# A scheduled attention-plus-scan kernel: the third bank of a three-bank score tile may be lent to VectorE, and the plan's seeds are drawn anew

## The chip, the core and the metric

The kernel runs on one core of one Trainium2 chip. The metric is the device time of one execution in microseconds (us): 775.2 us is the median of the three runs before the change (774.59 to 775.41). Five engines run side by side, each with its own queue: TensorE (PE in the profile), VectorE (DVE), ScalarE (ACT), GpSimd (POOL) and SyncE (SP), which here only issues DMAs.

## What is computed

Two independent layers over 2048 positions and 640 channels, whose outputs stand side by side. A is a diagonal complex state-space layer, B an attention with 32 query heads of width 20 that share one key and one value head:

```
A:  h = Lam_bar * h + B_bar @ x[t];  y[t] = 2 * Re(C @ h) + Dskip * x[t]
B:  q = (x @ wq) in 32 heads of 20;  k = x @ wk;  v = x @ wv
    p = softmax(q k^T / sqrt(20));   out = (p v, heads joined) @ wo
out = concat(A, B)
```

## The kernel before

**The bulk of the work is the exponential.** Attention is cut into 32 groups (4 blocks of 512 queries, 8 groups of 4 heads each). A group has 64 units; a unit is one head's 512 queries against 128 keys: a 128x512 tile of scores that needs an exponential. That makes 2048 units. A unit goes one of two ways:

- **By ScalarE.** TensorE writes two or three units into one PSUM tile, `R0` (three banks) and `R1` (two banks) in turn (`TILES = (3, 2)`), and one ACTIVATE with Exp (line 1243) turns the whole tile into bf16 probabilities in `P`. One PV matmul a unit then adds to `PV`.
- **By VectorE, a "D unit".** TensorE writes one unit into a bank of its own, `B0` or `B1`. One tensor_scalar (`dx_op`, line 1248) adds an offset, clamps at zero and converts to int16, whose bits read as bf16 approximate the exponential. Three shifted copies (`sh_op`, line 1253), each over up to three units, and four PV matmuls, with value rows scaled for each shift, average the error out. So a D unit costs VectorE one pass out of PSUM and three in SBUF, and TensorE four PV matmuls where a ScalarE unit needs one.

PSUM has eight banks: three for `R0`, two for `R1`, one for `PV`, and two for `B0` and `B1`. Those two B banks are shared by the D units and by every other matmul that needs PSUM: the query projections, the state-space input products (`sa`, lines 870 to 890), the state-space outputs (`sy`, y_tile, whose 13 or 12 matmuls hold one bank from the first to the last), and the output projection (`proj`).

**The order of instructions is made by a planner in the kernel file** when it is built. `main` keeps a clock for each engine and a list of candidates: the next fill of `R0` or `R1` ("fill"), the next exponential ("ex"), the next D unit ("dx"), shifts ("sh"), PV matmuls ("pv") and the heads of some background threads ("bg"). Each is offered with the time at which it could begin, plus a bias and some noise; the smallest goes next. Each operation then waits, on the chip, for the semaphores of the buffers that it reads and writes (`Plan.deps`), so a plan that is wrong about a duration shows up as a wait.

A fill may take a D unit with it. `want_d` decides: it wants the next of nine `Pd` slots to be free, a free B bank (`bank(None)`), no background thread that has waited for a bank longer than its patience (`starved`), VectorE's backlog below a limit, and the bank ready in time. `owner` tells for each of the two B banks who holds it; `d_group` allows 16 D units a group. `pick` chooses the units, `fill_op` makes the matmuls: 32 key rows each and three or four side by side, or, where two units stand alone, two of 64 rows. `R0c` is the dependency key of the third bank of `R0`; a three-unit fill and a three-unit exponential write and read both `R0` and `R0c`, and a two-unit one only `R0`.

The limits, patience and noise are drawn anew 64 times over the work by `vary`, from `random.Random(seed)` with the list `SEEDS`. Changing one entry, or one draw in `vary`, changes the whole order behind it.

Of the kernel before, what the change touches and what calls it, by code (L numbers as in the profile page):

```python
# [9 lines left out]
ALU = mybir.AluOpType  # L10
# [203 lines left out]
def dve_t(n, rate=1.0):  # L214
    return n / (960.0 * rate) + 0.07
# [28 lines left out]
class _Kernel:  # L244
# [17 lines left out]


    TURNS = 64
    SEEDS = (1006, 2007, 3008, 4004, 5008, 6003, 0, 8008, 9006, 0, 11003, 0, 13002, 14008, 0, 16002, 17003,
# [3 lines left out]

    def __init__(self, nc, t):  # L270
        self.nc, self.t = nc, t
# [21 lines left out]
    def alloc(self):  # L293
# [3 lines left out]
                  for i, n in enumerate(self.TILES)]  # L297
        self.PV = self.scope.enter_context(nc.psum_tensor("PV", [128, 512], FP32))
        self.BB = self.scope.enter_context(nc.psum_tensor("B", [128, 512 * self.BANKS], FP32))
        self.B = [self.BB[:, 512 * i:512 * i + 512] for i in range(self.BANKS)]  # L300
        self.p.psum.update(["R0", "R0c", "R1", "R1b", "PV", *(f"B{i}" for i in range(self.BANKS))])
        self.sb("xbT", [128, NC, S], BF16)
        self.sb("KT", [128, 2, S], BF16)
# [798 lines left out]
    def vary(self, seed):  # L1102

        r = self.rng = random.Random(seed)
        self.backlog = r.choice((2.5, 3.0, 3.5, 4.0, 5.0))
        self.spared = r.choice(((0.02, 0.02, 0.02), (0.05, 0.15, 0.02), (0.1, 0.3, 0.02), (0.02, 0.3, 0.02)))
        self.after = r.choice((0.1, 0.15, 0.2)), r.choice((0.35, 0.4, 0.5))
        self.few, self.wait, self.noise = r.choice((1, 1, 2)), r.choice((0.15, 0.25, 0.35)), r.choice((0.0, 0.05, 0.1))

        self.starved = dict(sy=r.choice((0.0, 1.0, 4.0, 99.0)), sa=r.choice((2.0, 99.0)),  # L1110
                            proj=r.choice((0.0, 1.0, 4.0, 99.0)),
                            qt=r.choice((0.0, 1.0, 4.0, 99.0)))
        self.open, self.first = r.choice((0.6, 0.7)), r.choice(("sy", "proj", None))

    def main(self):
        K, p = self, self.p
        NG = self.NQB * self.NGG
# [30 lines left out]
        def scan_open():  # L1148
# [2 lines left out]
        self.normed, self.projected, self.dense = set(), set(), set()  # L1151
        rest = self.rest
        done = lambda k=None: all(x == 64 for x in taken) and not any(k in (None, n % 2) for n, _ in tiles)
        fins = self.last_ops([lambda: done(0), lambda: done(1), lambda: done() and cur["raw"] == NG and not (any(owner) or sy or norm or proj),
                              lambda: done() and cur["raw"] == NG],
                             lambda gg: NG - self.NGG + gg in self.normed and not (gg == self.NGG - 1 and sy))
        threads = [("rest", rest), ("norm", norm), ("dense", dense), ("proj", proj), ("qt", qt), ("qr", qr), ("sy", sy), ("sa", sa), ("su", su), ("sr", sr), ("sc", sc_), ("sx", sx), *fins]
        owner = [None, "rest"]
        rest[-1].done = lambda: owner.__setitem__(1, None)
        holds, since = {}, {}  # L1160

        def bank(o):

            f = [i for i in range(2) if owner[i] is None]
            if not f:
                return None
            return min(f, key=lambda i: p.begin("pe", (), (f"B{i}",)))
# [6 lines left out]
        def pick(size, with_d):  # L1174

            g = next(i for i in range(NG) if taken[i] < 64)
            out, d = [], None
            heads = set()
            if size == 2 and not with_d and sum(len(x) for x in left[g]) > 8:
                for i in (0, 2):  # L1180
                    out.append((g, max((i, i + 1), key=lambda j: (bool(left[g][j]), -made(g, j), (taken[g] // 5 + j) % 2))))
                if all(left[g][j] for _, j in out):
                    return out, d
                out = []
            if with_d:
                gd = d_group(g)
                j = min(range(4), key=lambda j: (dcount[gd][j], made(gd, j), -len(left[gd][j])))
                if left[gd][j]:
                    d = (gd, j)
                    heads.add(j)  # L1190
            for gx in (g, g + 1):
                if gx >= NG or gx not in qt_done:
                    break
                for j in sorted(range(4), key=lambda j: (made(gx, j), -len(left[gx][j]), (j - taken[gx]) % 4)):
                    if j not in heads and left[gx][j] and len(out) < size:
                        out.append((gx, j))
                        heads.add(j)
            return out, d
# [13 lines left out]
                g += 1  # L1212
            return g if g < NG and g in qt_done and sum(dcount[g]) < self.QUOTA else None

        def want_d(g, t, n_tile):
            if not (g > 0 or taken[g] >= 24) or d_group(g) is None:
                return False
            if dunit_left.get(cur["d"] - self.DUNITS, 0) or bank(None) is None:
                return False
            if any(owner) and any(t - x > self.starved[name] * (name != "qt" or len(self.qsent) > 0) for name, x in since.items()):  # L1220
                return False
            return (backlog(t) <= self.backlog - 0.5 * n_tile
                    and p.begin("pe", (), (f"B{bank(None)}",)) <= t + self.spared[n_tile])

        def fill_op(n, out, d):
            lst, reads, writes = [], set(), ([f"R{n % 2}"] if out else []) + ["R0c"] * (len(out) == 3)
            units = list(out) + ([d] if d else [])
            wide = len({j // 2 for _, j in units}) == len(units)
            for i, (g, j) in enumerate(units):
                kc = left[g][j][-1]  # L1230
                lo, n_rows = (64 * (j // 2), 64) if wide else (32 * j, 32)
                dst = K.B[bank(None)][:, :] if i == len(out) else K.R[n % 2][:, 512 * i:512 * i + 512]
                lst.append(self.m1(dst, K.KT[lo:lo + n_rows, j % 2, 128 * kc:128 * kc + 128],
                                   K.QT[lo:lo + n_rows, g % self.QRING, :], True, True, (lo, 0), len(units)))
                reads |= {f"KT{j % 2}_{kc // 4}", f"QT{g % self.QRING}"}
            if d:
                writes.append(f"B{bank(None)}")
            return self.mms(lst, sorted(reads), writes, kind="QK")

        def ex_op(n, size):  # L1240
# [4 lines left out]

        def dx_op(n):
            u, x = n % self.DUNITS, holds[n]
            return Op("dve", lambda e: e.tensor_scalar(K.Pd[:, 0, u, :], K.B[x][:, :], self.d_off, 0.0, op0=ALU.add,  # L1248
                                                       op1=ALU.max), [f"B{x}"], [f"Pd{u}_0"], occ=dve_t(512))

        def sh_op(us, i):
            a, b = us[0][0], us[-1][0] + 1
# [38 lines left out]
        while True:  # L1291
# [8 lines left out]
            def offer(kind, o, bias, thread=None, arg=None):  # L1300
                cand.append((p.begin(o.eng, *o.keys(), o.accum) + bias + self.noise * self.rng.random(), len(cand), kind, o, thread,
                             arg))
# [3 lines left out]
            if cur["fill"] < cur["act"] + 2 and any(x < 64 for x in taken) and not early:  # L1306
                n = cur["fill"]
                g = next(i for i in range(NG) if taken[i] < 64)
                if g in qt_done:
                    t = p.begin("pe", (), (f"R{n % 2}",))  # L1310
                    out, d = pick(self.TILES[n % 2], want_d(g, t, n % 2))
                    o = fill_op(n, out, d)
                    t_fill = p.begin("pe", o.reads, o.writes)
                    t_fill = (t_fill, t_fill + self.after[n % 2])
                    offer("fill", o, -self.noise, arg=(out, d))
                    t = p.clock["pe"]
                    if d is None and want_d(g, t, 2):
                        d = pick(0, True)[1]
                        if d:
                            offer("fill", fill_op(n, [], d), 0.2, arg=([], d))  # L1320
            full = bool(tiles) and tile_left.get(tiles[0][0] - self.PTILES, 0) > 0
            if tiles:
                n, out = tiles[0]
# [80 lines left out]
                if o.done is not None:  # L1404
                    o.done()
            elif kind == "fill":
                out, d = arg
                self.units += len(out) + (d is not None)
                if out:
                    n = cur["fill"]  # L1410
# [5 lines left out]
                if d:  # L1416
                    g, j = d
                    taken[g] += 1
                    dcount[g][j] += 1
                    due[g][j] += 3  # L1420
                    dunits.append((cur["d"], (g, j, left[g][j].pop())))
                    holds[cur["d"]] = int(o.writes[-1][1])
                    owner[holds[cur["d"]]] = "D"
                    cur["d"] += 1
            elif kind == "ex":
# [80 lines left out]
```

## Time and profile before

| what | value |
|---|---|
| median of 3 runs | 775.2 us (774.59 to 775.41) |
| the profiled execution, its own time | 775.14 us |
| its span, first to last instruction | 773.2 us (1.9 us lie around it) |
| ScalarE busy | 757.0 us, 98% of the span |
| VectorE busy | 702.4 us, 91% |
| TensorE matmuls busy | 697.5 us, 90% |
| GpSimd busy | 441.0 us, 57% |
| exponentials (line 1243) | 325 of three banks, 328 of two |
| D units (line 1248) | 417, at 683 ns |
| shifts (line 1253) | 522, at 530 ns on average |
| granted TensorE clock | 0.989 |

Busy times are unions: two overlapping instructions of one engine count once. The mean of a group is that of an instruction from its own start to its own end, so overlapping ones have means that add up to more than the busy time. "Idle before" is the engine's idle time ahead of an instruction, with what ended it. Windows are in us from the start of the span.

### The profile page before, as it was taken

Reading aid. Unit: us, or ns where it says so; the run is one execution under the profiler, and the core shown is the slowest. Engines: PE = TensorE matmul, PEld = TensorE weight load, DVE = VectorE, ACT = ScalarE, POOL = GpSimd, SP = SyncE. Lnnn points to the kernel's source line nnn. Section 1 sums busy time; section 2 is a strip of 40 time slices with the busy share of each in tenths; the row PEclk is TensorE's granted clock in tenths of the full one; section 3 lists DMA queues with packets and bytes.
Section 4 is the critical chain, followed back from the end, with each engine's and each line's share of the span. In section 5 each row is a group of like instructions: output and inputs, shape, how many; then the busy total and the mean of one; then the engine's idle time right before and its main releaser. Section 6 shows DMA issues by size and latency. Waiting matters only on the chain.

```text
span 773.2 us, 16569 instructions
## 1 busy us (share of the span) xinstructions
PE 697.5 (90%) x6495; PEld 213.1 (28%) x6495; DVE 702.4 (91%) x1232; ACT 757.0 (98%) x686; POOL 441.0 (57%) x865
## 2 busy tenths in 40 slices
PE   5899887888889999998899999988899999889988
PEld 1322222222223333222223333222233332233323
DVE  6689999999997989899999788999989899998986
ACT  7999999999999999999999999999999999999995
POOL 4705753699997212499865300599992489940040
PEclk9799999999999999998999999999999999999999
DMA  8466101000020000210002010310000211000010
GB/s 186 86 149 132 38 15 49 16 16 15 1 57 29 30 23 32 51 50 15 15 10 61 30 40 17 65 42 23 2 23 22 62 40 38 2 19 21 28 42 35
DMA packets 61146, 31.49 MB, mean 41 GB/s; under 512 B 41478, under 2 KB 61070, under 8 KB 61070
## 3 DMA queue, kind: packets, MB, share of 16 engines
q1 hardware_dynamic: 58928, 30.12, 15.4%
q8 instruction: 52, 0.85, 0.5%
q10 hardware_dynamic: 2142, 0.32, 0.3%
q14 instruction: 24, 0.20, 0.1%
HBM read 9.21 MB, written 12.69 MB: 28 GB/s over the span
## 4 chain that ended last, share of the span: by engine, by line
ACT 69%; POOL 10%; DVE 10%; PE 8%; SPq 1%; issue 1%; DMA 1%; DVEq 0%; POOLq 0%
ACT P L1243 69%; POOL tm L906 4%; DVE Pd L1253 4%; POOL W L906 3%; PE R L418 3%; DVE Pd L1248 3%; PE PV L418 3%; PE B L418 2%; POOL uh L906 2%; SPq L399 1%; DVE hh L917 1%; DVE tm L890 1%; DMA xbT<-in_B_x_dram 1%; POOL tm L847 0%; DVE mabs L529 0%
## 5 line engine op out<-in xcount | busy, mean ns | idle before, releaser
L1243 ACT ACTIVATE P<-R 128x1536 bf16<-128x1536 f32 (+1 forms) x653 | 739.2, 1421 | 3.3 <-PE B L418 1.1
L1248 DVE TENSOR_SCALAR Pd<-B 128x512 int16<-128x512 f32 x417 | 282.3, 683 | 32.3 <-PE B L418 29.2
L418 PE MATMUL R<-QT,KT 32*128 32x512 bf16 (+1 forms) x1631 | 257.5, 389 | 56.7 <-ACT P L1243 42.7
L1253 DVE TENSOR_SCALAR Pd<-Pd 128x1536 int16<-128x1536 int16 (+2 forms) x522 | 259.9, 530 | 1.2
L418 PE MATMUL PV<-P,VP 128*32 128x512 bf16 x1631 | 256.2, 389 | 0.8 <-DVE Pd L1248 0.4
L418 PE MATMUL PV<-Pd,VP 128*32 128x512 bf16 x1668 | 252.6, 386 | 3.0 <-DVE OTr L1286 2.1
L906 POOL TENSOR_TENSOR tm<-hh,cs 128x128 bf16<-128x128 f32 x320 | 164.8, 537 | 23.4 <-DVE hh L917 8.9
L418 PE MATMUL B<-QT,KT 32*128 32x512 bf16 x417 | 161.6, 388 | 0.0
L418 PEld LDWEIGHTS R<-QT,KT 32*128 32x128 bf16 (+1 forms) x1631 | 64.1, 91 | 298.1 <-ACT P L1243 268.4
L906 POOL TENSOR_TENSOR W<-tm 128x128 bf16<-128x128 bf16 x160 | 91.9, 597 | 89.8 <-PE B L418 85.9
L906 POOL TENSOR_TENSOR uh<-tm 128x128 bf16<-128x128 bf16 x160 | 81.1, 527 | 63.7 <-DVE tm L890 59.6
L418 PEld LDWEIGHTS PV<-Pd,VP 128*32 128x32 bf16 x1668 | 59.1, 94 | 64.4 <-issue 38.3
L418 PEld LDWEIGHTS PV<-P,VP 128*32 128x32 bf16 x1631 | 59.2, 94 | 61.0 <-issue 45.9
L1000 POOL TENSOR_TENSOR OTd<-OTd,rwide 128x128 bf16<-128x128 bf16 x80 | 33.7, 448 | 67.8 <-DMA OTd<-o_rows 65.9
L890 DVE TENSOR_TENSOR tm<-B,cs 128x1024 bf16<-128x1024 f32 x40 | 48.5, 1213 | 3.6 <-PE B L418 3.4
L418 PE MATMUL B<-CGre,W 128*128 128x384 bf16 (+1 forms) x160 | 46.5, 305 | 0.8 <-POOL W L906 0.8
L418 PE MATMUL B<-CGim,W 128*128 128x384 bf16 (+1 forms) x160 | 45.6, 299 | 0.0
L847 POOL TENSOR_SCALAR tm<-W,sc 128x128 f32<-128x128 bf16 x40 | 30.7, 779 | 20.0 <-DVE CGre L849 12.5
L917 DVE TENSOR_TENSOR_SCAN hh<-sc,hini,uh 128x512 f32<-128x512 f32 x30 | 39.5, 1318 | 0.0
L418 PEld LDWEIGHTS B<-QT,KT 32*128 32x128 bf16 x417 | 37.8, 91 | 0.0
L418 PE MATMUL B<-xaT,BTim 128*128 128x512 bf16 x100 | 30.4, 384 | 0.6 <-DVE tm L890 0.4
L418 PE MATMUL PV<-cs,VP 128*128 128x512 bf16 x88 | 30.5, 390 | 0.0
(149 smaller groups left out, 414.1 us busy)
## 6 DMA issues: line engine op xcount, KB each, us to landing
o_rows<-OTr SPq DMA_DIRECT2D x32, 128.0 KB, 1.7
QT<-q_rows SPq DMA_DIRECT2D x30, 128.0 KB, 2.2
q_rows<-Qd SPq DMA_DIRECT2D x16, 160.0 KB, 2.8
OTd<-o_rows SPq DMA_DIRECT2D x16, 160.0 KB, 3.2
out_dram<-ystage SPq DMA_DIRECT2D x16, 160.0 KB, 1.8
out_dram<-ostage SPq DMA_DIRECT2D x12, 160.0 KB, 1.8
P<-in_B_wq_dram SPq DMA_DIRECT2D x1, 800.0 KB, 5.9
WO<-in_B_wo_dram SPq DMA_DIRECT2D x4, 200.0 KB, 3.5
```

Source lines behind the costliest of these rows:

```text
L399: return e.dma_start_transpose(out_ap, in_ap)
L418: ins = e.matmul(o() if callable(o) else o, lhsT=l, rhs=r, start=st, stop=sp, skip_group_check=True, **kw)
L847: pool(lambda e, y=y, c=c, gy=gy, i=i: e.tensor_scalar(K.ctmp[:, i:i + 128], y[:, i:i + 128], sc[:, gy, c:c + 1], None, op0=ALU.mult), key ...
L890: dve(lambda e, k=k, h=h: e.tensor_tensor(K.tm[:, 2 * k:2 * k + 2, :], bass.AP(tensor=K.BB, offset=512 * int(h.key[1]), ap=[[512 * self.BA ...
L906: put(lambda e, c0=c0, end=end: e.tensor_tensor(out[:, c0:end], a[:, c0:end], b[:, c0:end], op), reads, [writes + h], n, gate=None if i el ...
L917: dve(lambda e, ri=ri, ini=ini: e.tensor_tensor_scan(K.hh[:, ri, :], dec, K.uh[:, ri, :], ini, ALU.mult, ALU.add), ["sc", *(f"uh{ri}{h}" f ...
L1000: ops.append(Op("pool", lambda e, c=c, m=m: e.tensor_tensor(K.OTd[:, m, c], K.OTd[:, m, c], K.rwide[:, c], ALU.mult), rw + [f"OTe{dd}" for ...
L1243: return Op("act", lambda e: e.activation(dst, K.R[n % 2][:, 0:512 * size], ACT.Exp, scale=self.exp_scale), [f"R{n % 2}"] + ["R0c"] * (siz ...
L1248: return Op("dve", lambda e: e.tensor_scalar(K.Pd[:, 0, u, :], K.B[x][:, :], self.d_off, 0.0, op0=ALU.add, op1=ALU.max), [f"B{x}"], [f"Pd{ ...
L1253: return Op("dve", lambda e: e.tensor_scalar(K.Pd[:, i, a:b, :], K.Pd[:, 0, a:b, :], float(self.SHIFTS[i]), 0.0, op0=ALU.subtract, op1=ALU ...
```

## The change

Three things change, and all of them change the plan; no instruction becomes another kind.

1. **The third bank of `R0` becomes a third bank for D units**, `B[2]`, with the key `R0c`. If the regular `want_d` refuses a D unit for a three-bank tile, it is asked again with `lent=True`. That form does not ask for a free B bank and does not look at starved threads; it asks that the third bank is not already lent (`owner[2]`), that the last group is not far along (`t_left`), that VectorE's backlog is below the limit by another 0.5 or 1.0 us (`lend`), and that `R0c` is free in time. If it agrees, the fill writes two units for ScalarE into banks 0 and 1 and one D unit into bank 2. The exponential of that tile has two banks.
2. **While the bank is lent** (until the VectorE pass that reads it has been put into the plan), the next fill of `R0` has two units, not three. Once that pass is in the plan, the next three-unit fill waits for it by its semaphore.
3. **`vary` draws `lend`** ahead of `open` and `first`, and `SEEDS` is a new list (58 of its 64 entries are not 0; before, 53).

```
+        self.B = [... for i in range(self.BANKS)] + [self.R[0][:, 1024:1536]]
+        self.bkeys = [f"B{i}" for i in range(self.BANKS)] + ["R0c"]
...
+        self.lend = r.choice((0.5, 1.0))
...
-        owner = [None, "rest"]
+        owner = [None, "rest", None]
...
+        def t_left():
+            return taken[NG - 1] < 40
+
-        def want_d(g, t, n_tile):
+        def want_d(g, t, n_tile, lent=False):
             if not (g > 0 or taken[g] >= 24) or d_group(g) is None:
                 return False
-            if dunit_left.get(cur["d"] - self.DUNITS, 0) or bank(None) is None:
+            if dunit_left.get(cur["d"] - self.DUNITS, 0):
                 return False
-            if any(owner) and any(t - x > self.starved[name] * ... for name, x in since.items()):
+            if lent:
+                return (self.lend < 9 and owner[2] is None and t_left() and backlog(t) <= self.backlog - 0.5 * n_tile - self.lend
+                        and p.begin("pe", (), ("R0c",)) <= t + self.spared[n_tile])
+            if bank(None) is None:
+                return False
+            if any(owner[:2]) and any(t - x > self.starved[name] * ... for name, x in since.items()):
                 return False
...
-                dst = K.B[bank(None)][:, :] if i == len(out) else K.R[n % 2][:, 512 * i:512 * i + 512]
+                dst = K.B[x][:, :] if i == len(out) else K.R[n % 2][:, 512 * i:512 * i + 512]
...
-                    out, d = pick(self.TILES[n % 2], want_d(g, t, n % 2))
-                    o = fill_op(n, out, d)
+                    size, x = self.TILES[n % 2] - (n % 2 == 0 and owner[2] is not None), bank(None)
+                    d = want_d(g, t, n % 2)
+                    if not d and size == 3 and want_d(g, t, 0, True):
+                        size, d, x = 2, True, 2
+                    out, d = pick(size, d)
+                    o = fill_op(n, out, d, x)
```

More of the change, by code (lines that the diff above doesn't have):

```diff
@@ L264 @@
     TURNS = 64
-    SEEDS = (1006, 2007, 3008, 4004, 5008, 6003, 0, 8008, 9006, 0, 11003, 0, 13002, 14008, 0, 16002, 17003,
[3 rows of a table removed]
+    SEEDS = (3008, 4003, 5007, 6005, 7007, 8009, 9006, 10003, 0, 12001, 13005, 14006, 15009, 16007, 17005, 18006,
[4 rows of a table added]
     def __init__(self, nc, t):
@@ L299, in alloc @@
         self.BB = self.scope.enter_context(nc.psum_tensor("B", [128, 512 * self.BANKS], FP32))
-        self.B = [self.BB[:, 512 * i:512 * i + 512] for i in range(self.BANKS)]
+        self.B = [self.BB[:, 512 * i:512 * i + 512] for i in range(self.BANKS)] + [self.R[0][:, 1024:1536]]
+        self.bkeys = [f"B{i}" for i in range(self.BANKS)] + ["R0c"]
         self.p.psum.update(["R0", "R0c", "R1", "R1b", "PV", *(f"B{i}" for i in range(self.BANKS))])
@@ L1153, in main @@
         done = lambda k=None: all(x == 64 for x in taken) and not any(k in (None, n % 2) for n, _ in tiles)
-        fins = self.last_ops([lambda: done(0), lambda: done(1), lambda: done() and cur["raw"] == NG and not (any(owner) or sy or norm or proj),
+        fins = self.last_ops([lambda: done(0), lambda: done(1), lambda: done() and cur["raw"] == NG and not (any(owner[:2]) or sy or norm or proj),
                               lambda: done() and cur["raw"] == NG],
@@ L1213, in d_group @@
             return g if g < NG and g in qt_done and sum(dcount[g]) < self.QUOTA else None
-        def want_d(g, t, n_tile):
+        def t_left():
+            return taken[NG - 1] < 40
+        def want_d(g, t, n_tile, lent=False):
             if not (g > 0 or taken[g] >= 24) or d_group(g) is None:
                 return False
-            if dunit_left.get(cur["d"] - self.DUNITS, 0) or bank(None) is None:
+            if dunit_left.get(cur["d"] - self.DUNITS, 0):
                 return False
-            if any(owner) and any(t - x > self.starved[name] * (name != "qt" or len(self.qsent) > 0) for name, x in since.items()):
+            if lent:
[3 more added lines that the diff above has]
+                return False
+            if any(owner[:2]) and any(t - x > self.starved[name] * (name != "qt" or len(self.qsent) > 0) for name, x in since.items()):
                 return False
@@ L1223, in want_d, with fill_op @@
                     and p.begin("pe", (), (f"B{bank(None)}",)) <= t + self.spared[n_tile])
-        def fill_op(n, out, d):
+        def fill_op(n, out, d, x):
             lst, reads, writes = [], set(), ([f"R{n % 2}"] if out else []) + ["R0c"] * (len(out) == 3)
@@ L1236, in fill_op @@
             if d:
-                writes.append(f"B{bank(None)}")
+                writes.append(K.bkeys[x])
             return self.mms(lst, sorted(reads), writes, kind="QK")
@@ L1247, in dx_op @@
             u, x = n % self.DUNITS, holds[n]
+            key = K.bkeys[x]
             return Op("dve", lambda e: e.tensor_scalar(K.Pd[:, 0, u, :], K.B[x][:, :], self.d_off, 0.0, op0=ALU.add,
-                                                       op1=ALU.max), [f"B{x}"], [f"Pd{u}_0"], occ=dve_t(512))
+                                                       op1=ALU.max), [key], [f"Pd{u}_0"], occ=dve_t(512))
         def sh_op(us, i):
@@ L1310, in main @@
                     t = p.begin("pe", (), (f"R{n % 2}",))
-                    out, d = pick(self.TILES[n % 2], want_d(g, t, n % 2))
-                    o = fill_op(n, out, d)
+                    size, x = self.TILES[n % 2] - (n % 2 == 0 and owner[2] is not None), bank(None)
[4 more added lines that the diff above has]
+                    o = fill_op(n, out, d, x)
                     t_fill = p.begin("pe", o.reads, o.writes)
                     t_fill = (t_fill, t_fill + self.after[n % 2])
-                    offer("fill", o, -self.noise, arg=(out, d))
+                    offer("fill", o, -self.noise, arg=(out, d, x))
                     t = p.clock["pe"]
@@ L1319, in main @@
                         if d:
-                            offer("fill", fill_op(n, [], d), 0.2, arg=([], d))
+                            offer("fill", fill_op(n, [], d, bank(None)), 0.2, arg=([], d, bank(None)))
             full = bool(tiles) and tile_left.get(tiles[0][0] - self.PTILES, 0) > 0
@@ L1406, in main @@
             elif kind == "fill":
-                out, d = arg
+                out, d, x = arg
                 self.units += len(out) + (d is not None)
@@ L1421, in main @@
                     dunits.append((cur["d"], (g, j, left[g][j].pop())))
-                    holds[cur["d"]] = int(o.writes[-1][1])
+                    holds[cur["d"]] = x
                     owner[holds[cur["d"]]] = "D"
```

7 rows, old and new, of the table SEEDS are left out of this document.

## The prediction

> **What bounds the kernel now.** I read the page's first two parts, then the groups of each engine with forms kept apart, then the waits and the windows.
>
> ```profile
> span 773.2 us, 16569 instructions
> PE 697.5 (90%) x6495; PEld 213.1 (28%) x6495; DVE 702.4 (91%) x1232; ACT 757.0 (98%) x686; POOL 441.0 (57%) x865
> DVE  6689999999997989899999788999989899998986
> ACT  7999999999999999999999999999999999999995
> ```
>
> ScalarE is the bound. It is full in every slice but the first and the last. The rest of the span, 773.2 - 757.0 = 16.2 us, is nearly all head and tail. The groups, forms kept apart, say what fills it:
>
> ```profile
> L1243 ACT ACTIVATE P<-R 128x1536 bf16<-128x1536 f32 x325 | 530.6, 1633 | 3.2 <-PE B L418 1.1 <-PE R L418 0.8 <-PE PV L418 0.6
> L1243 ACT ACTIVATE P<-R 128x1024 bf16<-128x1024 f32 x328 | 395.9, 1211 | 0.1
> L1248 DVE TENSOR_SCALAR Pd<-B 128x512 int16<-128x512 f32 x417 | 282.3, 683 | 32.3 <-PE B L418 29.2
> ```
>
> The exponentials have 325 x 3 + 328 x 2 = 1631 units in 653 tiles, and in front of them stands 3.3 us of idle time. The 417 D units are the rest of the 2048. So the end moves with the number of units that ScalarE must take and with the number of tiles, and hardly with anything else. The page's merged row of line 1243 is busy 739.2 us. A bank more costs 1633 - 1211 = 422 ns, so the tiles' fixed share is (739.2 - 1631 x 0.422) / 653 = 0.078 us. Check: a three-bank tile takes 1.344 us of ScalarE, a two-bank tile 0.922, and 325 and 328 of them are 739 us again. (Their own means are longer since neighbours overlap.)
>
> VectorE is the second full engine, and its largest wait is the third row above: 29.2 us before `dx` passes, for a fill that was not there. That wait is what the change could turn into work. The windows show where it lies:
>
> ```profile
> core 0: us, PE busy (x) PEld busy (x) DVE busy (x) ACT busy (x) POOL busy (x), PEclk, DMA share, GB/s
> 40.00:760.00 720.00, 657.96 (x6192) 197.95 (x6188) 669.55 (x1160) 717.93 (x635) 417.48 (x803) 1.00 0.13 35
> 240.00:320.00 80.00, 78.29 (x731) 26.83 (x727) 70.51 (x136) 79.89 (x72) 21.50 (x48) 1.00 0.08 26
> 400.00:480.00 80.00, 77.74 (x710) 25.28 (x711) 68.67 (x126) 80.00 (x73) 22.94 (x49) 1.00 0.12 36
> 480.00:560.00 80.00, 70.34 (x676) 20.43 (x673) 77.57 (x132) 80.00 (x72) 65.17 (x126) 1.00 0.14 34
> ```
>
> Columns: length, then busy time and count of each engine. Between 40 and 760 us VectorE is idle 720 - 669.55 = 50.5 us. In 240 to 320 and 400 to 480 it is idle 9.5 and 11.3 us; these are the stretches in which state-space outputs and projections hold B banks. In 480 to 560 it is idle only 2.4 us. TensorE stands the other way round: idle 1.7 and 2.3 us in the first two, 9.7 in the third.
>
> **The change, part by part.**
>
> *What a D unit is worth.* Each unit that leaves ScalarE saves 0.422 us. It costs VectorE (282.3 + 259.9) / 417 = 1.30 us (one pass and its share of the shifts; the shifts' group is busy 259.9 us on the page), beside ScalarE's work as long as VectorE has room. It costs TensorE three more PV matmuls. The tile view of `PV` has 299.0 us of union for 3333 matmuls between 40 and 760 us, or 0.09 each, so 0.27 us; by the busy time of the PV group of D units alone (252.6 us for 1668) it is 0.45 us. Both lie in TensorE's 62 us of idle time in that stretch; where that cover is missing they delay background matmuls first, since a fill goes ahead of them.
>
> *How many fills can lend.* In the trace every D unit rides on a fill: 228 of the 325 three-bank fills and 189 of the 328 two-bank fills have one. So 97 three-bank fills go without. 91 of these lie between 40 and 755 us. In the 2.26 us behind such a fill (one pair of tiles, 1.344 + 0.922), VectorE is idle for more than 0.3 us in 26 cases and for more than 0.6 us in 13. With the rest VectorE is full, and the stricter backlog limit must refuse. I take 26 lends that are asked for in earnest, and 13 units as their net gain: those after which VectorE has half of a unit's 1.30 us to spare; the others take the place of a regular D unit a little later. The ends: 0 units (all displaced), and 28.2 us, VectorE's wait for D fills in 40 to 760 us, / 1.30 = 22 units.
>
> *What the shorter tiles cost.* Besides the lending tile, the next `R0` tile is short too if VectorE's pass is not planned by then. I take half again: 40 short tiles in all, an estimate between 26 and the 97. Units: 1631 - 13 = 1618 = 2.5 x T - 40, so T = 663, ten tiles more. That is 10 x 0.078 = +0.8 us. The Trainium skill (ScalarE: Activation LUTs, What ACT_TABLE_LOAD costs) gives an ACTIVATE with immediates 186 ns plus 0.833 ns an element, with 93 ns of overlap back to back. By that the fixed share would be 93 ns and the ten tiles +0.9 us; the rows above have 0.078, and they decide.
>
> *The wait that is added.* A three-unit fill now can wait for the `dx` pass that reads the lent bank. Behind it on TensorE's queue stand the PV matmuls and the fill of `R1`; ScalarE waits for the fill when its current tile ends. The trace has no such wait, but its nearest rows are the fills that waited for a B bank:
>
> ```profile
> PE R L418 <- DVE Pd L1248: 2.1, 6, 0.6
> PE R L418 <- DVE tm L890: 1.5, 4, 0.6
> PE R L418 <- DVE Pd L1253: 1.3, 3, 0.5
> ```
>
> (us in total, times, longest.) 4.9 us over 417 D fills is 0.012 us each; for 40 short tiles that is 0.5 us. Lower end 0 (the pass is always done), upper end half of the 40 at the rows' mean of 4.9 / 13 = 0.38 us, 7.6 us. I take 0.5, since the planner knows this dependency as it knows those.
>
> *The seeds.* They move every instruction, and no row prices them. They can't change a duration; they change how many D units are found. All of VectorE's idle time of 50.5 us would be 38 units (-16 us). The other way, windows of 40 us have 17 to 27 D units, and if the quiet ones lost one each, 18 units would be +8 us. I take 0, and 7 units (3 us) either way into the range.
>
> *Small edits.* `owner[:2]` and the new parameter `x` cost no instruction. The tail's own use of bank 2 comes after `t_left` has stopped lending.
>
> **Sum.** -13 x 0.422 + 0.8 + 0.5 = -4.2 us. Against the profiled execution's own 775.14 us that is 770.9, and since the median is 0.06 above it, **771.0 us**.
>
> **The rivals.**
>
> *A. The lent units only displace regular ones, or TensorE has no room for them: no change.* For: in the two stretches where VectorE has room TensorE is busy 97 to 98%, with 4.0 us idle in 160 us, room for 9 units at 0.45; elsewhere VectorE is full. Then some 4 units are won, -1.7 + 0.8 + 0.5 = -0.4 us: 774.8. Against: the longest PE idle group is fills that wait for ScalarE, and much of what fills TensorE there is background that can move. The Trainium skill (Perfetto Trace Analysis, Identifying the Most-Contended Engine) says that the busy share of matmuls is a bad measure of how full TensorE is, and that the busy share of weight loads is a better one; here that is 34% and 32% in those stretches against 26% in 480 to 560. By that rule this rival loses weight; no run here shows it yet.
>
> *B. Slower: the coupling of VectorE to `R0`.* A late `dx` used to delay a D unit; now it delays ScalarE's own tile. The place is the `R0` fill behind a lend, the price 0.38 us. ScalarE has little cushion: a short tile keeps it busy for 0.922 us instead of 1.344, in which TensorE must refill the other tile. The point from which it decides is (5.5 - 0.8) / 40 = 0.12 us a short tile. At half of the 40 with 0.38 us: -4.7 + 7.6 = +2.9 us, 778.1. For it: VectorE is 93% busy in 40 to 760, so it will often be behind. Against: only 3.3 us of idle time stands before 653 exponentials today, with the same sort of coupling by B banks.
>
> *C. Faster than forecast: the bank was the true limit*, and the full 22 units are won: -9.3, with 60 short tiles (T = 668, +1.2) and 0.8 of waits: -7.3, 767.9; with the seeds' 3 us more, 764.9.
>
> **How the numbers follow.** Forecast (768.5 to 773.6) 0.42, C 0.15, A 0.19, B 0.24. The range reaches from C with its seeds to B with 1 us of what the seeds may add: 764.9 to 779.0; it leaves out some 0.15 to 0.2. A measurement of this kernel can tell about 0.2% (1.6 us) from no change. So faster 0.57, same 0.19, slower 0.24.
>
> **What would show it.** In the profile after: a new group `Pd<-R` at VectorE's `dx` line, some 26 to 60 of it; all `dx` together about 430; fewer three-bank and more two-bank exponentials, about 663 in all; VectorE's wait for fills down from 29.2 to about 15 us; idle time before the exponentials still below 5 us. The prediction is wrong if all `dx` together stay near 417 (A), if idle time before exponentials, ended by fills that waited for VectorE, grows by over 5 us (B), or if VectorE's busy share goes to 95% and beyond (C).

## The result, and the profile after

The changed kernel takes 769.9 us (768.96 to 770.03, four runs) against 775.3 us of the kernel before in the same session: a ratio of 0.993, 95% interval 0.9913 to 0.9947. It is 5.4 us faster; 4.2 us were forecast. The profiled execution took 768.96 us, with a span of 767.2 us (773.2 before).

The first two fences have the engine line and the costliest ScalarE and VectorE groups of the changed kernel, forms kept apart. Columns as before: busy us and mean ns, then idle us ahead of it and what ended it. The line numbers have moved: 1243 is 1254 now, 1248 is 1260, 1253 is 1265.

```profile
PE 684.0 (89%) x6466; PEld 213.1 (28%) x6529; DVE 709.6 (92%) x1228; ACT 751.7 (98%) x700; POOL 429.1 (56%) x865
```

(The trace has 6466 matmuls beside 6529 weight loads, one a matmul; the 63 that are missing make TensorE's 684.0 us too small, so it is not compared with the 697.5 before.)

```profile
L1254 ACT ACTIVATE P<-R 128x1536 bf16<-128x1536 f32 x284 | 466.8, 1644 | 2.2 <-PE R L420 1.6 <-PE B L420 0.5
L1254 ACT ACTIVATE P<-R 128x1024 bf16<-128x1024 f32 x382 | 437.5, 1212 | 0.7 <-PE R L420 0.5
...
L1260 DVE TENSOR_SCALAR Pd<-B 128x512 int16<-128x512 f32 x385 | 260.8, 682 | 24.2 <-PE B L420 21.4
...
L1260 DVE TENSOR_SCALAR Pd<-R 128x512 int16<-128x512 f32 x46 | 31.4, 682 | 2.1 <-PE R L420 1.8
```

The new row is the last: 46 D units were read out of the lent bank. With the 385 in B banks that makes 431, 14 more than before. Three-bank exponentials fell from 325 to 284, two-bank ones rose from 328 to 382, and with one single-bank tile there are 667 for 1617 units. ScalarE is as full as before. The page's merged rows of the exponentials, before and after:

```profile
L1243 ACT ACTIVATE P<-R 128x1536 bf16<-128x1536 f32 (+1 forms) x653 | 739.2, 1421 | 3.3 <-PE B L418 1.1
L1254 ACT ACTIVATE P<-R 128x1024 bf16<-128x1024 f32 (+1 forms) x667 | 733.9, 1395 | 3.0 <-PE R L420 2.1
```

They are busy 5.3 us less, and their idle time is 3.0 us, before 3.3. So of the span's 6.0 us, 5.3 are exponential time. TensorE's granted clock, 0.996 against 0.989 in the two profiled executions, does not explain them: a slower TensorE would show in the idle time before the exponentials, and that differs by 0.3 us.

Where did the 14 units come from? The windows of the changed kernel, in two of the stretches that the prediction shows:

```profile
240.00:320.00 80.00, 78.06 (x746) 26.75 (x751) 72.94 (x130) 79.87 (x76) 35.05 (x75) 1.00 0.08 27
400.00:480.00 80.00, 78.47 (x738) 26.59 (x740) 71.56 (x133) 79.99 (x74) 20.94 (x49) 1.00 0.13 38
```

(TensorE, weight loads, VectorE, ScalarE, GpSimd.) VectorE was busy 70.5 and 68.7 us in these two stretches; now 72.9 and 71.6. Counted in the trace by the start of the pass, 240 to 320 us has 45 D units of which 10 are lent (before 40), 400 to 480 has 43 with 6 lent (before 41), and the first 80 us have 28 with 5 lent (before 22). In 480 to 560, where VectorE was full, there are 49 as before, 3 of them lent. So the two stretches in which B banks are held and VectorE had time gained seven, and the first 80 us six; elsewhere gains and losses of one to five units come to one.

### The profile page after: what moved, and what is told of

Its sections match the earlier page's. It is cut to its first block, busy times and chain, and to the rows that moved or that the text cites. A ratio compares the mean times of both kernels' runs of the same rounds, so it can differ in the third digit from the quotient of the medians.

```text
span 767.2 us, 16567 instructions
## 1 busy us (share of the span) xinstructions
PE 684.0 (89%) x6466; PEld 213.1 (28%) x6529; DVE 709.6 (92%) x1228; ACT 751.7 (98%) x700; POOL 429.1 (56%) x865
## 4 chain that ended last, share of the span: by engine, by line
ACT 76%; DVE 10%; PE 10%; POOL 1%; SPq 1%; DMA 1%; issue 0%
ACT P L1254 76%; PE R L420 4%; DVE Pd L1265 4%; PE PV L420 4%; DVE Pd L1260 4%; PE B L420 2%; SPq L401 1%; DVE hh L919 1%; DVE tm L892 1%; DMA xbT<-in_B_x_dram 1%; POOL tm L849 1%; POOL uh L908 1%; POOL tm L908 0%; DVE mabs L531 0%; DVE CGim L851 0%
## 5 line engine op out<-in xcount | busy, mean ns | idle before, releaser
L1254 ACT ACTIVATE P<-R 128x1024 bf16<-128x1024 f32 (+1 forms) x667 | 733.9, 1395 | 3.0 <-PE R L420 2.1
L420 PE MATMUL R<-QT,KT 32*128 32x512 bf16 (+1 forms) x1663 | 261.0, 386 | 58.7 <-ACT P L1254 45.3
L1260 DVE TENSOR_SCALAR Pd<-B 128x512 int16<-128x512 f32 x385 | 260.8, 682 | 24.2 <-PE B L420 21.4
L908 POOL TENSOR_TENSOR tm<-hh,cs 128x128 bf16<-128x128 f32 x320 | 161.8, 527 | 25.2 <-DVE hh L919 16.3
L420 PE MATMUL B<-QT,KT 32*128 32x512 bf16 x385 | 148.0, 385 | 0.0
L908 POOL TENSOR_TENSOR W<-tm 128x128 bf16<-128x128 bf16 x160 | 85.6, 556 | 19.3 <-PE B L420 15.0
L420 PEld LDWEIGHTS B<-QT,KT 32*128 32x128 bf16 x385 | 34.8, 91 | 0.0
L1260 DVE TENSOR_SCALAR Pd<-R 128x512 int16<-128x512 f32 x46 | 31.4, 682 | 2.1 <-PE R L420 1.8
L420 PE MATMUL B<-xaT,BTim 128*128 128x512 bf16 x93 | 28.2, 384 | 1.2 <-issue 0.8
```

The source lines that it names most:

```text
L420: ins = e.matmul(o() if callable(o) else o, lhsT=l, rhs=r, start=st, stop=sp, skip_group_check=True, **kw)
L908: put(lambda e, c0=c0, end=end: e.tensor_tensor(out[:, c0:end], a[:, c0:end], b[:, c0:end], op), reads, [writes + h], n, gate=None if i el ...
L1254: return Op("act", lambda e: e.activation(dst, K.R[n % 2][:, 0:512 * size], ACT.Exp, scale=self.exp_scale), [f"R{n % 2}"] + ["R0c"] * (siz ...
```

## The experiments

### Is a late pass on the lent bank dear?

Two kernels with the order of the changed one untouched. In the first the pass of each lent D unit is cut in four; in the second, that of the regular unit behind each lent one.

```
+            slow = x == 2                               # late_lent
+            slow = x < 2 and holds.get(n - 1) == 2      # late_b
+            def fn(e):
+                w = 128 if slow else 512
+                for i in range(0, 512, w):
+                    r = e.tensor_scalar(K.Pd[:, 0, u, i:i + w], K.B[x][:, i:i + w], ...)
+                return r
```

> The changed kernel with its order untouched, but each of the 46 VectorE passes that read the lent bank is cut into four passes of 128 columns, which should take some 0.3 us longer together (46 x 0.3 = 14 us more VectorE work, of about 39 us idle). Theory (lending pays by units, the coupling of VectorE to the three-bank tile is loose): a late pass on the lent bank costs about what a late pass on a B bank does, so +1 to +4 us over the changed kernel's 769.9, and within 1.5 us of late_b. Rival (the coupling is tight and only the plan's timing keeps it from showing): each late pass delays a fill of R0, 46 x 0.15 to 0.3 us, +7 to +14 us, and at least 4 us above late_b; idle time before exponentials grows by as much.

> The control: the same order, and the same cut into four passes for the 46 D units in B0 or B1 that come directly behind the lent ones. The same extra VectorE work at nearly the same places, but on banks that ScalarE never reads. Theory and rival agree here: +1 to +4 us over 769.9, from the fills that wait for a B bank or PV matmuls that wait for shifts. If it costs as much as late_lent, the lent bank is no dearer than a B bank.

Measured: late_lent 772.35 us, ratio to the kernel before 0.9974 (0.9961 to 0.9986); late_b 770.58 us, ratio 0.9954 (0.9937 to 0.9971). The cut passes, from the groups of late_lent:

```profile
L1265 DVE TENSOR_SCALAR Pd<-R 128x128 int16<-128x128 f32 x184 | 40.1, 277 | 1.9 <-PE R L420 1.8
```

184 pieces are busy 40.1 us where 46 whole passes were busy 31.4: 0.19 us more each, so the probe was weaker than meant (8.7 us in all, not 14). TensorE's waits show what became of it: fills of `R` that waited for a VectorE pass out of PSUM, first late_lent, then late_b.

```profile
PE R L420 <- DVE Pd L1265: 4.0, 12, 1.2
```

```profile
PE R L420 <- DVE Pd L1265: 3.3, 7, 1.1
```

Twelve waits against seven, 0.7 us more in all. A row does not tell which bank was waited for. Counted in the traces by the tile that the pass read, fills waited for the lent bank for 1.4 us in 5 waits in late_lent, 1.2 us in 3 in late_b and 0.8 us in 2 in the changed kernel; the rest of these waits were for B banks.

The difference in time is 1.8 us by the medians, just over the 1.5 us that the theory allowed, and the intervals of the two ratios overlap. Where both kernels were granted 0.993 of TensorE's clock (five and three executions), the means are 1.2 us apart. So a lent pass that is 0.19 us late costs about 1.8 / 46 = 0.04 us more than one on a B bank, and by the outer ends of the two intervals (0.9986 - 0.9937, or 3.8 us) not more than 0.08. Had each late pass held up a fill by its whole 0.19 us, the two would be 8.7 us apart: the tight form of the rival is out, a weaker one is not. The coupling of VectorE to ScalarE's tile is there and is loose in this plan.

### Lending and seeds, each alone

The changed kernel without lending, and the old seeds with it:

```
         self.lend = r.choice((0.5, 1.0))
+        self.lend = 9.0                       # off_same_seeds: never lends
```

```
-    SEEDS = (3008, 4003, 5007, ...            # on_old_seeds, and the draw of lend
+    SEEDS = (1006, 2007, 3008, ...            # moved behind that of open and first
```

> The changed kernel and its new seeds with lending switched off (the draw of lend is kept, its value set to 9). Its instruction stream has 395 D units, 36 fewer, and 662 exponentials instead of 667. Theory (the gain is the extra D units that lending made room for): 36 x 0.43 - 5 x 0.05 = +15 us of ScalarE time, about 785 us. Rival (the new seeds alone brought the gain): it stays below the kernel before, 775.3. A caution on record: these seeds were drawn for plans that lend, so a result near 785 doesn't show that no seeds without lending reach 770.

> The list of seeds of the kernel before, and lending on (the draw of lend moved behind the others, so that the draws before the first lend are those of before). 426 D units (70 lent) against 417, and 680 exponentials against 653. By ScalarE's account alone -9 x 0.432 + 27 x 0.053 = -2.5 us. If the lists matter as off_same_seeds made likely, the idle time of a plan that nobody drew comes on top: 8 to 20 us before exponentials, so 780 to 792 us, slower than before although it has more D units. If it is faster than 774, the lists hardly matter.

Measured: off_same_seeds 786.8 us, ratio 1.0159 (1.0146 to 1.0172); on_old_seeds 787.0 us, ratio 1.0142 (1.0127 to 1.0157). Each half of the change, under a list that was not drawn for it, makes the kernel slower. In the profile off_same_seeds has 395 D units, its exponentials are busy 749.3 us and idle before them 5.1 us: it lost units. on_old_seeds has 426 D units, more than the kernel before, and its exponentials are busy 739.3 us, as before; it lost by waits, as its ScalarE groups show:

```profile
L1253 ACT ACTIVATE P<-R 128x1024 bf16<-128x1024 f32 x416 | 446.9, 1157 | 6.3 <-PE PV L419 4.9 <-PE R L419 0.9
L1253 ACT ACTIVATE P<-R 128x1536 bf16<-128x1536 f32 x263 | 415.8, 1581 | 7.1 <-PE B L419 3.5 <-PE R L419 2.8 <-PE PV L419 0.2
```

13.4 us of idle time before exponentials instead of 3.3. "PV" as the releaser (5.1 us here, 0.6 in the kernel before) means that the exponential's `P` slot still had a PV matmul to come. These two runs say that a list of seeds fits one kind of plan. They do not say what lending is worth, since neither list was drawn for its setting.

on_old_seeds says even less of lending than was meant. The planner's noise comes from the same generator as the draws of `vary`, so one draw more shifts the noise from the first turn on. In the trace its order leaves that of the kernel before at 29 us, while its first pass on a lent bank starts at 46.3 us. So this run has other noise as well as lending. off_same_seeds keeps the draw, and its order leaves that of the changed kernel only at the first lend, whose pass starts at 34.0 us.

### Lists that nobody drew

Two plain lists (1100, 2100, ... and 1101, 2101, ...), each with lending on and off.

> An undrawn list of seeds (1100, 2100, ... 64100), lending on. 421 D units (76 of them lent) and 685 exponentials; beside plain0_off 382 and 667. Theory by ScalarE's account: on minus off = -39 x 0.432 + 18 x 0.053 = -16 us. Rival (coupling): most of that comes back as idle time before exponentials, which is at least 10 us longer with lending, and on minus off is between -6 and +4 us.

> The undrawn list of seeds 1100, 2100, ... with lending off: 382 D units and 667 exponentials in its instruction stream (with lending on: 421 and 685; that run gave 799.9 us, with 24 us of idle time before exponentials). Theory by ScalarE's account, 16 us more of ScalarE time than with lending and idle time before exponentials alike (within 6 us): about 810 to 816 us. Rival (lending brings idle time): idle time before exponentials 10 us or more below that with lending, and the time 796 to 806 us.

> A second undrawn list (1101, 2101, ...), lending on: 426 D units (68 lent), 677 exponentials. By the account of the theory, 9 us of ScalarE time less than plain1_off. Idle time before exponentials well above the 3 us of the two drawn plans, some 15 to 25 us, since nobody chose this list: about 785 to 798 us.

> The second undrawn list, lending off: 403 D units, 658 exponentials. Theory: 5 to 13 us slower than plain1_on, ScalarE 9 us busier, idle time before exponentials alike. Rival: lending's idle time eats that, and the two are within 4 us.

| list | D units on / off | time on | time off | exponentials busy on / off | idle before them on / off |
|---|---|---|---|---|---|
| plain0 | 421 / 382 | 799.9 us | 799.7 us | 743.2 / 755.7 | 24.1 / 9.9 |
| plain1 | 426 / 403 | 792.7 us | 803.7 us | 739.1 / not compared | 19.7 / not compared |

(The profiled execution of plain1_off was granted 0.836 of TensorE's clock against 0.97 in the others and took 812.2 us, so its rows are not compared.) For plain0 the rival was right and the theory (16 us faster with lending) wrong: ScalarE had 12.5 us less to do, and 14.2 us came back as idle time. These are the groups, with lending and then without:

```profile
L1254 ACT ACTIVATE P<-R 128x1024 bf16<-128x1024 f32 x426 | 447.4, 1135 | 10.1 <-PE PV L420 6.1 <-PE R L420 2.8 <-PE B L420 0.8
L1254 ACT ACTIVATE P<-R 128x1536 bf16<-128x1536 f32 x258 | 399.8, 1550 | 14.0 <-PE B L420 5.3 <-PE R L420 4.4 <-PE PV L420 3.3
```

```profile
L1255 ACT ACTIVATE P<-R 128x1536 bf16<-128x1536 f32 x333 | 533.2, 1601 | 9.0 <-PE PV L420 4.1 <-PE B L420 2.9 <-PE R L420 1.7
L1255 ACT ACTIVATE P<-R 128x1024 bf16<-128x1024 f32 x333 | 393.1, 1180 | 0.9 <-PE B L420 0.5 <-PE PV L420 0.3
```

By the waits of the two kernels, late fills (`R` and `B`) held the exponentials up for 13.3 us with lending and 5.1 without, PV matmuls for 9.4 and 4.4. TensorE's fills that had waited for a VectorE pass out of PSUM grew too, with lending and then without:

```profile
PE R L420 <- DVE Pd L1260: 6.3, 15, 1.1
PE R L420 <- DVE Pd L1261: 1.8, 6, 0.4
```

By the tile that the pass read, 2.4 us of the 6.3, in 6 waits, were for the lent bank and 3.9, in 9, for B banks. So the coupling by the lent bank is there, and it is the smaller part of what came back.

The granted clock has a part in both of these runs. By the traces' records TensorE was granted half of its clock in several stretches of 3 to 17 us each, together 48 us of plain0_on, 51 us of plain0_off and 17 us of the kernel before. Of the idle time before exponentials, 7.0 and 4.8 us (1.6 in the kernel before) lie in such stretches or within 2 us behind them. This may be a part of why both are slower than the kernel before; it hardly tells them apart.

For plain1 the time moved as the theory said, 11.1 us. Lending found 39 and 23 more D units in the plans that nobody chose, and in one of them it lost as much again by waits.

### Seeds drawn with equal effort, with and without lending

The fair question is what a list reaches that was looked for with lending off. Two searches of my own, by the planner's own end time, each run once with lending and once without, with the same effort. Only `SEEDS` and, for off, the line `self.lend = 9.0` differ from the changed kernel.

> The changed kernel with a third list of seeds, drawn by a search of its own (five best prefixes kept at each of the 64 places, ten seeds tried behind each), lending on. 434 D units (81 lent), 680 exponentials. Smaller search than that of the two kernels, so idle time before exponentials of 3 to 12 us: 770 to 782 us.

> The same search with the same effort and lending off: 409 D units, 656 exponentials. This is the fair form of the question that off_same_seeds left open. Theory (lending brings units that a list without it can't find): slower than redrawn3_on by 25 x 0.42 - 24 x 0.08 = 8.6 us of ScalarE time, with idle time within 4 us of it: 4 to 12 us slower. Rival (the gain was the draw of the seeds): within 2 us of redrawn3_on.

> A fourth list of seeds by the same kind of search from other numbers (four best prefixes kept), lending on: 427 D units (88 lent), 685 exponentials. About 772 to 782 us, with idle time before exponentials of 4 to 10 us.

> The same search with lending off: 408 D units, 656 exponentials. Theory: by ScalarE's account 19 x 0.42 - 29 x 0.08 = 5.7 us more than redrawn103_on, of which 3.4 us may come back as idle time, as it did between the two runs of the first redrawn pair: 1 to 7 us slower than redrawn103_on. Rival (the draw alone decides, and the first pair was luck): within 1 us of it, or faster.

| pair | D units on / off | time on | time off | ratio to before, on | ratio to before, off |
|---|---|---|---|---|---|
| redrawn3 | 434 / 409 | 774.0 us | 780.0 us | 0.9992 (0.9983 to 1.0002) | 1.0062 (1.0050 to 1.0074) |
| redrawn103 | 427 / 408 | 780.8 us | 782.0 us | 1.0069 (1.0055 to 1.0083) | 1.0080 (1.0065 to 1.0095) |

In the first pair lending is worth 6.0 us, clear of both intervals and inside the theory's 4 to 12. Its parts are in the merged rows of the exponentials, with lending and then without:

```profile
L1252 ACT ACTIVATE P<-R 128x1024 bf16<-128x1024 f32 (+1 forms) x680 | 734.3, 1352 | 6.3 <-PE B L418 4.7
L1253 ACT ACTIVATE P<-R 128x1536 bf16<-128x1536 f32 (+1 forms) x656 | 743.4, 1410 | 3.2 <-PE B L418 2.2
```

They are busy 9.1 us less (8.6 were worked out), with 3.1 us more of idle time before them. VectorE's wait for fills is the mechanism to be seen, first with lending, then without:

```profile
L1258 DVE TENSOR_SCALAR Pd<-B 128x512 int16<-128x512 f32 x353 | 238.1, 681 | 20.8 <-PE B L418 17.8
L1258 DVE TENSOR_SCALAR Pd<-R 128x512 int16<-128x512 f32 x81 | 55.2, 681 | 2.3 <-PE R L418 1.5
```

```profile
L1259 DVE TENSOR_SCALAR Pd<-B 128x512 int16<-128x512 f32 x409 | 276.9, 683 | 38.3 <-PE B L418 35.4
```

35.4 us of waiting for fills without lending, 19.3 with it. In the second pair the difference is 1.1 us and the intervals overlap: it lies between the theory's 1 to 7 us and the rival's "within 1 us" and decides nothing. The parts of its profiled executions look alike, only smaller: exponentials busy 738.8 against 743.5 us, idle time before them 7.6 against 5.8, and VectorE's wait for fills 27.8 against 36.0. But where TensorE's granted clock was much the same (0.973 to 0.979), three executions with lending took 781.05 to 782.01 us and five without took 780.76 to 782.53, so no difference is left to be seen. None of the four lists reaches the changed kernel's 769.9, so the list that came with the change is the better draw, and no version that was run beats it.

## Why the prediction was right

**What bounds the kernel** held: ScalarE is 98% busy before and after, and 5.3 us of the span's 6.0 are exponential time.

**Net D units**, forecast 13: 14. The number came out, but the way to it was off in two parts that cancel. I took 26 lends and half of them as net gain. There were 46 lends, and regular D units fell by 32 (417 to 385), so fewer than a third (14 of 46) were net; the new list of seeds is in these counts too. Both the number of lends and the displacement were undersized: I had counted the fills behind which VectorE was seen idle in the old plan, and the new plan is another one, with a lend of its own wherever its limits allow it. That the two errors cancelled is luck.

**Short tiles**, forecast 663 exponentials in all, ten more: 667, fourteen more. Carry-over, a second short `R0` tile behind a lend, hardly happened: about 50 `R0` tiles are not three banks wide and 46 of them lend; I had taken one in two.

**ScalarE's sum.** By the prediction's prices the measured counts give -14 x 0.422 + 14 x 0.078 = -4.8 us; measured -5.3. Both prices came from the kernel before alone. Solved from both busy times, 739.2 and 733.9 us, they are 0.432 us a bank and 0.053 us a tile; the expectations use these. So the term for the tiles rests on a price that the runs leave between 0.05 and 0.08 us.

**Added wait**, forecast +0.5 us: idle time before exponentials went from 3.3 to 3.0 us. Rival B, the coupling, hardly showed in this plan (two fills waited for the lent bank, 0.8 us together), and late_lent shows that there is cushion for most of 0.19 us in each lent pass. It is not a phantom: in plain0, a plan that nobody chose, idle time took back all that lending brought. The seeds are what keeps it away here. That part of the prediction ("I take 0" for the seeds, with 3 us either way) was the weakest, and that it did no harm is luck too: on_old_seeds and off_same_seeds show that a list that does not fit costs 11 to 12 us against the kernel before, four times the 3 us that I allowed.

**Rival A** (no room on TensorE) fell. In 240 to 320 and 400 to 480 us TensorE's matmuls were busy 78.3 and 77.7 of 80 us, and yet 5 and 2 more D units with three PV matmuls more each went in, with TensorE busy 78.1 and 78.5 now. In the forecast background work was to give way. In number nothing did, in sum: weight loads, one a matmul, rose from 727 to 751 and from 711 to 740 there. That agrees with the rule of the Trainium skill cited in the prediction (Perfetto Trace Analysis, Identifying the Most-Contended Engine): weight loads were busy 26.8 and 25.3 us there and are 26.8 and 26.6 now, a third of the stretch.

**VectorE's wait for fills** was forecast to fall to about 15 us; it fell from 29.2 to 21.4 in B banks plus 1.8 in the lent one. That is 6 us of the 14 that I expected to go.

**What stays open.** How the 5.4 us divide between lending and a luckier draw. At equal effort lending was worth 6.0 us once and 1.1 us once (unclear), so the change's 5.4 can be all lending, or some of it the better search. Two pairs do not settle it, and with the plain lists (0 and 11.1 us) four pairs differ among themselves by more than the 5.4 us in question. How much search went into the two given lists is not known.

## What to carry to other kernels

When one engine is full from end to end, count what it must do (here units x 0.42 us plus tiles x 0.08 us) and ask only how the change moves those counts and the idle time in front of them; the forecast of -4.2 us came within 1.2 us of the result. A buffer that one engine has for itself can be lent to another if its reader is seldom late, but each lend also displaces regular work: here three to five lends made one net unit in the plans that were searched for (14 of 46, 25 of 81, 19 of 88). And where a plan is found by search, judge an option only with lists searched for it and, with equal effort, without it; run under a list that was not drawn for it, each of the two halves of this change looked like a loss of 11 to 12 us.

## What the runs showed that I had not expected

How far plans differ. With the same kinds of instruction and lending off, lists of seeds range from 775 us (the kernel before) over 780 (a search) to 804 (a plain list), with D units from 382 to 417 and idle time before exponentials from 3 to 10 us where it could be read.

In the plans with much idle time, exponentials waited for their `P` slot (9.4 us in plain0 with lending, 4.4 without), a wait of 0.6 us in the kernel before. A two-bank tile takes a whole one of the ten slots, so more short tiles leave fewer units in flight; that this is why it doubled is argued, not shown, and no run with more slots was made. Against it, 6.5 of the 9.4 us are four waits in one place, between 56 and 67 us.

A VectorE pass out of PSUM over 128 columns took 277 ns from start to end where one of 512 took 682: four pieces were busy 40.1 / 46 = 0.87 us against 0.68, so cutting a pass in four costs 0.19 us and not 0.43, because neighbours overlap.
